# Summing v in two halves of 64 rows on Trainium2: a packed-attention kernel with a gated feed-forward

## The chip, the cores and the metric

One Trainium2 chip, one core of it. The metric is the time of one execution of the whole kernel on the device, in microseconds; lower is better. TensorE (PE) multiplies matrices and loads its weights in instructions of their own (PEld), VectorE (DVE) and ScalarE (ACT) read what it wrote to PSUM, GpSimd (POOL) works in SBUF, and SyncE (SP) issues the transfers.

## The reference

Eight batches of eight heads, 576 tokens, 64 numbers a head. 32 packing vectors p attend to the tokens, and the tokens then attend to the 32 packed vectors. The result goes through a gated feed-forward.

```
scale = 1.0 / np.sqrt(q.shape[-1])
def sm_attn(qq, kk, vv):
    s = scale * np.matmul(qq, kk.transpose(0, 1, 3, 2))
    s = s - np.max(s, axis=-1, keepdims=True)
    a = np.exp(s)
    a = a / (np.sum(a, axis=-1, keepdims=True) + 1e-09)
    return np.matmul(a, vv)
p_packed = sm_attn(p, k, v)                  # 8 x 8 x 32 x 64
out = sm_attn(q, p_packed, p_packed)         # 8 x 8 x 576 x 64
x = out.transpose(0, 2, 1, 3).reshape(B * S, H * D)
return (x @ w_a) * (x @ w_b) @ w_out         # 4608 x 512
```

## The kernel before

The batches are worked off one after the other (b = 0 to 7). Batches 0 and 1 go through a feed-forward written out slot by slot (the loops over `mm1`, lines L410 to L429); batches 2 to 7 go through a loop of periods of some 7 us each, `period`, with products at L799, the second feed-forward product at L758 as filler between them, and the weights of the next periods folded with the packed vectors in `make_g` (L813 on PE, L819 to L828 on ACT, DVE and POOL). The attention of batch b + 1 is cut into steps, which are put into the slots and periods of batch b by tables written out by hand (START, PLAN_0, PLAN, STEPS). All engines work in program order: the manual schedule keeps the order in which the code is written.

`stage1(b, e)` is the first attention of four heads (e = 0 and 1 take every other head). Its steps are: the scores (L270), the maximum (L276), the exponentials (L288), the reciprocal of the sum (`rs`, L295), the transposes that put tokens on partitions (L309 to L312, into `a1T`), and the sums of v (L319), which are scaled into `pp` (L325). It runs 16 times in all. `turned` (L256, L258) later turns `pp` into `ppT`, which `stage2` and `make_g` use.

The sums of v have five chunks of tokens, four of 128 and one of 64. For each chunk, head r of four multiplies `a1T` (128 rows by 32 columns, the weights) with `vt` (128 rows by 64 columns) and adds into partitions 32r to 32r + 31 of one bank. The profile shows each such fp32 matmul as two records, so a call leaves 40. In a form "128\*32" the array is used with 128 rows and 32 columns, in "64\*32" with 64 rows and 32 columns, in "128\*128" whole.

PSUM: `bank_pair(True)` is the one pair of banks called `s`, which the scores, the transposes, the sums of v, the second attention's scores and `turned` take in turn from batch 1 on; `bank_pair()` is one of two pairs called `m`, and `bank()` one of two single banks called `x`. So the scores of e = 1 (L270, step S1) write `s` only after DVE has read the sums of e = 0 out of it (L325). In batches 3 to 7 step S1 stands right behind `make_g`, one period after the sums of e = 0.

Of the kernel before, what the change touches and what calls it, by code (L numbers as in the profile page):

```python
# [12 lines left out]
ALU = mybir.AluOpType  # L13
# [6 lines left out]
def tile_packed_attn_gated_ffn(  # L20
# [20 lines left out]
    nc = tc.nc  # L41
    B, H, S, D = q.shape
    J = p.shape[2]
    DM, DF = w_a.shape
    DO = out.shape[1]
    P = 128
# [8 lines left out]
    NT = 5  # L55
# [37 lines left out]
    def bank():  # L93
        return ps_x.tile([P, 512], F32, name="x")

    def bank_pair(s=False):
        return ps_s.tile([P, 2, 512], F32, name="s") if s else ps_m.tile([P, 2, 512], F32, name="m")

    def work(b, name, shape, tag=None):
        if b == 0:  # L100
            return scratch.tile(shape, F32, name=name)
        return wk.tile(shape, F32, name=tag, bufs=2 if tag == "t1" else 1)
# [89 lines left out]
    def xT_cols(b, key, u, h, cols=slice(0, HS)):  # L192
        return xTs[b, key][h // R][64 * u:64 * u + 64, h % R, cols]
# [66 lines left out]
    pp, paired, a2f_of, banks_of = {}, [False], {}, {}  # L260

    def stage1(b, e):


        s = bank_pair(b or e == 0)
        first = b < 2
        parts = [(0, 0, 0, HS)] + ([(1, TR, 0, 2 * P), (1, 0, 2 * P, TR)] if first else [(1, 0, 0, HS)])
        for u, c, t, n in parts:
            for r in range(R):
                nc.tensor.matmul(  # L270
                    out=s[J * r:J * r + J, u, c:c + n], lhsT=pT[64 * u:64 * u + 64, 2 * r + e, :],
                    rhs=xT_cols(b, "k", u, 2 * r + e, slice(t, t + n)), start=True, stop=True)
        s = s[:, :, 0:HS]
        yield
        nmx = sm.tile([P, 1], F32, name="nmx")
        nc.vector.tensor_reduce(out=nmx, in_=s, axis=AXY, op=ALU.max)  # L276
        nc.vector.tensor_scalar(out=nmx, in0=nmx, scalar1=-scale, scalar2=None, op0=ALU.mult)
        if b > NB:
            yield
        a1 = work(b, f"a1_{e}", [P, S], "t1")  # L280
        rs = sm.tile([P, 1], F32, name="rs")
        if first:
            exps = [(a1, s, rs)]
        else:
            rs2 = sm.tile([P, 1], F32, name="rs2")
            exps = [(a1[:, 2 * TR:S], s[:, :, 0:2 * P], rs), (a1[:, 0:2 * TR], s[:, :, 2 * P:HS], rs2)]
        for dst, src, acc in exps:
            nc.scalar.activation(  # L288
                out=dst.rearrange("p (u t) -> p u t", u=2), in_=src, func=AF.Exp, bias=nmx, scale=scale, accum_out=acc)
        yield  # L290
        if first:
            nc.vector.tensor_scalar(out=rs, in0=rs, scalar1=1e-9, scalar2=None, op0=ALU.add)
        else:
            nc.vector.tensor_scalar(out=rs, in0=rs, scalar1=rs2, scalar2=1e-9, op0=ALU.add, op1=ALU.add)
        nc.vector.reciprocal(out=rs, in_=rs)  # L295
        yield
        a1T = work(b, f"a1T_{e}", [P, NT, P], "t2")
        rest = 2 * P if first else 0
        chunks = [P * i + ((HS + TR) * u if first else 2 * TR + 2 * P * u) for i in range(2) for u in range(2)]
        if b or e:  # L300
            pair = bank_pair(b)
            tp, tq = pair[:, 0, :], pair[:, 1, :]
        else:
            tp, tq = bank(), bank()
        if b == 0:
            chunks = [(HS + TR) * u + i for i in range(2) for u in range(2)]
        step = 1 if b else 2
        for i, c in enumerate(chunks):
            nc.tensor.transpose(tp[:, P * i:P * i + P], a1[:, c:c + step * (P - 1) + 1:step], ident)  # L309
        nc.tensor.transpose(tq[0:64, 0:P], a1[:, rest:rest + 2 * TR], ident)  # L310
        nc.scalar.copy(out=a1T[:, 0:4, :].rearrange("p i t -> p (i t)"), in_=tp)
        nc.scalar.copy(out=a1T[0:64, 4, :], in_=tq[0:64, 0:P])  # L312
        yield
        pps = bank_pair(True)[:, 0, :] if b else bank()
        vt = vts.pop((b, e))
        for i in range(NT):
            n = P if i < 4 else 64
            for r in range(R):
                nc.tensor.matmul(  # L319
                    out=pps[J * r:J * r + J, 0:D], lhsT=a1T[0:n, i, J * r:J * r + J],  # L320
                    rhs=vt[0:n, r, i, :], start=(i == 0), stop=(i == NT - 1))
        if e == 0:
            pp[b] = sm.tile([P, E + 1, D], F32, name="pp", bufs=1)
        for i in range(e, E + 1, E):
            nc.vector.tensor_scalar(out=pp[b][:, i, :], in0=pps[:, 0:D], scalar1=rs, scalar2=None, op0=ALU.mult)  # L325
        yield

    def stage2(b, e):
# [147 lines left out]
    def emit(b, plan, tasks={}):  # L476

        for name in plan.split():
# [16 lines left out]
            if what == "S":  # L495
                if e == 0:
                    st[b] = [stage1(b, 0), stage1(b, 1), stage2(b, 0), stage2(b, 1)]
                next(st[b][e])
            elif what == "s":
                next(st[b][2 + e], None)  # L500
            elif what == "r":
                next(st[b][e], None)
            elif what == "T":
                turn_p(p_nat.pop(n))
            elif what == "P":
                turned(ppT[:, b % 2:b % 2 + 2], pp.pop(b), b % 2)
            elif what in ("k", "q"):
                turn(what, n, e % 2) if b else turn_first(what, e)
            elif what == "Lk":
                load(k, "k", n, e % 2)  # L510
            elif what == "Lq":
                load(q, "q", n, e % 2)
            elif what == "Lv":
                load_v(n, e % 2)
            elif what == "Lp":
                load_p(n)
# [87 lines left out]
    for name in FIRST.split():  # L604
        what, i = name[0].lower(), int(name[1])
# [311 lines left out]
    start = slot[0]  # L917
# [16 lines left out]
    for n in range(LAST):  # L934
        b, ft = NB + n // NFT, n % NFT
# [18 lines left out]
    i, c0 = tiles[-1]  # L954
# [35 lines left out]
```

## Time and profile before

| | |
|---|---|
| median of 3 runs | 709.69 us (708.8 to 711.84) |
| span of the profiled execution | 708.6 us |
| PE busy | 698.7 us, 99% |
| weight loads (PEld) busy | 573.9 us, 81% |
| DVE busy | 447.6 us, 63% |
| ACT busy | 366.1 us, 52% |
| POOL busy | 410.8 us, 58% |

The span is that of one execution under the profiler. It lies 1.1 us under the median and just under the lowest of the three times, so a change of the span is taken as a change of the time. Busy shares are averages over the whole span; a busy PE is not one at its peak, since matmuls overlap.

### The profile page before, as it was taken

To read this page: it belongs to the slowest core of one execution; us is meant where nothing else is said; L and a number is where in the kernel's file an instruction comes from. 1 tells how busy PE (TensorE), PEld (TensorE's weight loads), DVE (VectorE), ACT (ScalarE), POOL (GpSimd) and SP (SyncE) were. 2 spreads that over 40 slices of the span, in tenths; PEclk is the share of its full clock that TensorE was granted. 3 is DMA by queue.
4 is the path that set the end of the run, shared out by engine and by line. 5 is a ranking of instruction groups with operands and counts; after the bars stand their busy time and mean duration, and the time that the engine had idled before them with its cause. 6 is when DMAs were issued, how large, how long until landed. Compare 5 with 4: busy or idle time off the path is not lost.

```text
span 708.6 us, 14190 instructions
## 1 busy us (share of the span) xinstructions
PE 698.7 (99%) x5556; PEld 573.9 (81%) x5556; DVE 447.6 (63%) x821; ACT 366.1 (52%) x735; POOL 410.8 (58%) x320
## 2 busy tenths in 40 slices
PE   8998999999999999999999999999999999999998
PEld 6486978897788888878888788788888888888886
DVE  4987655467355679665775678765785667754342
ACT  5987744544254555535554456545555446544510
POOL 0556652337244677746873589566775578856520
PEclk9999999999999999999999999999999999999999
DMA  9999954668254736456434563555245323133002
GB/s 316 382 217 317 270 98 84 191 154 286 65 131 161 173 88 168 124 138 148 138 94 123 157 175 94 123 172 154 77 113 167 105 90 120 61 122 116 1 1 74
DMA packets 176562, 102.56 MB, mean 145 GB/s; under 512 B 141936, under 2 KB 157936, under 8 KB 171120
## 3 DMA queue, kind: packets, MB, share of 16 engines
q1 hardware_dynamic: 176080, 101.08, 50.5%
q8 instruction: 43, 0.70, 0.4%
q10 hardware_dynamic: 416, 0.59, 0.2%
q14 instruction: 23, 0.19, 0.1%
HBM read 85.92 MB, written 15.73 MB: 143 GB/s over the span
## 4 chain that ended last, share of the span: by engine, by line
PE 90%; DMA 5%; ACT 2%; DVE 2%; SPq 1%; issue 0%; POOL 0%; DVEq 0%; ACTq 0%; POOLq 0%
PE x L758 37%; PE m L799 29%; PE m L410 8%; PE m L436 5%; PE x L813 5%; DMA raw<-in_moe_w_b_dram 2%; PE s L319 2%; PE s L334 1%; PE s L270 1%; DMA vt<-in_v_dram 1%; PE s L309 1%; DMA nat<-in_k_dram 1%; DMA wr<-w_kept 1%; PE x L389 1%; ACT raw L201 1%; DVE w_ab L212 0%
## 5 line engine op out<-in xcount | busy, mean ns | idle before, releaser
L758 PE MATMUL x<-wo,h_hi 128*128 128x512 f32 (+1 forms) x776 | 249.4, 391 | 0.2 <-ACT gs L819 0.2
L91 POOL TENSOR_TENSOR h_lo<-asb,h_hi 128x576 fp32r<-128x576 f32 x96 | 140.2, 1461 | 91.1 <-ACT h_hi L844 44.7
L758 PEld LDWEIGHTS x<-wo,h_hi 128*128 128x128 f32 x776 | 140.8, 188 | 22.3 <-ACT gs L819 1.2
L758 PE MATMUL x<-wo,h_lo 128*128 128x512 f32 (+1 forms) x388 | 152.1, 392 | 0.0
L91 POOL TENSOR_TENSOR G_lo<-gs,G_hi 128x640 fp32r<-128x640 f32 x72 | 113.0, 1575 | 30.8 <-ACT G_hi L834 30.5
L758 PEld LDWEIGHTS x<-wo,h_lo 128*128 128x128 f32 x388 | 72.9, 188 | 11.7
L91 POOL TENSOR_TENSOR A_lo<-gs,A_hi 128x256 fp32r<-128x256 f32 x36 | 27.1, 754 | 89.5 <-ACT A_hi L822 89.4
L881 DVE TENSOR_TENSOR d<-m,d 128x576 f32<-128x576 f32 (+1 forms) x73 | 54.0, 740 | 34.7 <-ACT d L877 33.9
L894 DVE TENSOR_TENSOR asb<-m,d 128x288 f32<-128x288 f32 x72 | 32.5, 451 | 66.7 <-ACT c L890 65.1
L890 ACT COPY c<-m 128x288 f32<-128x288 f32 x72 | 28.8, 399 | 78.3 <-PE m L799 78.3
L768 DVE TENSOR_TENSOR part<-x,part 128x512 f32<-128x512 f32 (+1 forms) x65 | 44.1, 678 | 38.8 <-PE x L758 38.8
L819 ACT COPY gs<-x 128x512 f32<-128x512 f32 x36 | 21.1, 587 | 83.3 <-PE x L813 80.2
L799 PE MATMUL m<-tx_hi,G_hi 128*128 128x288 f32 x216 | 63.8, 296 | 0.0
L799 PE MATMUL m<-tx_hi,G_lo 128*128 128x288 f32 x216 | 63.7, 295 | 0.0
L799 PE MATMUL m<-tx_lo,G_hi 128*128 128x288 f32 x216 | 63.3, 293 | 0.0
L834 ACT CAST G_hi<-gs 128x640 fp32r<-128x640 f32 x72 | 52.2, 730 | 15.1 <-POOL gs L828 14.5
L877 ACT COPY d<-m 128x576 f32<-128x576 f32 (+1 forms) x73 | 46.6, 639 | 20.2 <-PE m L799 18.6
L844 ACT CAST h_hi<-asb 128x576 fp32r<-128x576 f32 x72 | 49.0, 680 | 11.5 <-DVE asb L908 11.5
L799 PEld LDWEIGHTS m<-a_hi,G_hi 128*128 128x128 f32 x144 | 27.0, 187 | 31.9 <-issue 17.4
L828 POOL TENSOR_TENSOR gs<-gs 128x512 f32<-128x512 f32 x36 | 46.7, 1297 | 2.6 <-DVE gs L825 2.5
L799 PE MATMUL m<-a_hi,G_hi 128*128 128x288 f32 x144 | 47.1, 327 | 0.0
L410 PE MATMUL m<-a_hi,ghi 128*128 128x288 f32 x192 | 43.3, 307 | 2.8 <-ACT asb L422 2.8
(170 smaller groups left out, 1541.7 us busy)
## 6 DMA issues: line engine op xcount, KB each, us to landing
wr<-w_kept SPq DMA_DIRECT2D x36, 1024.0 KB, 5.1
nat<-in_k_dram SPq DMA_DIRECT2D x56, 144.0 KB, 5.2
nat<-in_q_dram SPq DMA_DIRECT2D x56, 144.0 KB, 5.3
vt<-in_v_dram SPq DMA_DIRECT2D x28, 256.0 KB, 3.7
out_dram<-part SPq DMA_DIRECT2D x27, 256.0 KB, 2.0
raw<-in_moe_w_a_dram SPq DMA_DIRECT2D x12, 512.0 KB, 9.3
raw<-in_moe_w_b_dram SPq DMA_DIRECT2D x12, 512.0 KB, 9.8
raw<-in_moe_w_out_dram SPq DMA_DIRECT2D x12, 512.0 KB, 6.4
```

The costliest lines, as they stand in the source:

```text
L91: return eng.tensor_tensor(out=dst, in0=src, in1=hi.bitcast(F32), op=ALU.subtract)
L410: nc.tensor.matmul(out=ps[:, half, 0:HS], lhsT=gt[:, kt, ft % 4, cols], rhs=at[:, kt, HS * half:HS * half + HS], start=(n == 0 and kt == 0 ...
L436: nc.tensor.matmul(out=o[:, cols], lhsT=ht[:, c0:c0 + P], rhs=wt[:, cols], start=(ft == 0 and n == 0), stop=(ft == NFT - 1 and n == 2))
L758: nc.tensor.matmul(out=o[:, cols], lhsT=ht[:, c0:c0 + P], rhs=wt[:, cols], start=(ft == fts[0] and n == 0), stop=end)
L768: nc.vector.tensor_tensor(out=parts[i][:, cols], in0=o[:, cols], in1=parts[i][:, cols], op=ALU.add)
L799: nc.tensor.matmul(out=bank[:, n % 2, 0:HS], lhsT=g, rhs=t, start=(first and i == 0), stop=(i == 2), skip_group_check=True)
L813: nc.tensor.matmul(out=gps[e][J * r:J * r + J, :], lhsT=ppT[rows, 2 * (b % 2), r, :], rhs=w[rows, r, :], start=True, stop=True)
L828: nc.gpsimd.tensor_tensor(out=gs[:, 2:4].rearrange("p a u f -> p a (u f)"), in0=gs[:, 0:2].rearrange("p a u f -> p a (u f)"), in1=s2.unsqu ...
L834: nc.scalar.copy(out=G_hi[:, n % 3], in_=gs[:, 1:6, n % 2])
L844: nc.scalar.copy(out=view(h_hi[ft]), in_=src)
L877: nc.scalar.copy(out=d[:, both], in_=X[:, both, 0:HS])
L881: nc.vector.tensor_tensor(out=d[:, both], in0=V[:, both, 0:HS], in1=d[:, both], op=ALU.add)
```

## The change

The sums of v take the four full chunks in halves of 64 rows: rows 0 to 63 add into the first bank of a pair, rows 64 to 127 into the second, and the last chunk of 64 rows into the first. DVE then scales the second bank's sums into a piece of `a1T` (which the matmuls have read by then) and adds that while it scales the first bank's. In batch 0 the sums take `s` and an `m` pair instead of two `x` banks. Lines behind the change stand four further down (L799 is L803, L813 is L817).

```
-        pps = bank_pair(True)[:, 0, :] if b else bank()
+        pps = bank_pair(b > 0 or e == 0)
         vt = vts.pop((b, e))
         for i in range(NT):
-            n = P if i < 4 else 64
             for r in range(R):
-                nc.tensor.matmul(
-                    out=pps[J * r:J * r + J, 0:D], lhsT=a1T[0:n, i, J * r:J * r + J],
-                    rhs=vt[0:n, r, i, :], start=(i == 0), stop=(i == NT - 1))
+                for g in range(2 if i < 4 else 1):
+                    rows = slice(64 * g, 64 * g + 64)
+                    nc.tensor.matmul(
+                        out=pps[J * r:J * r + J, g, 0:D], lhsT=a1T[rows, i, J * r:J * r + J],
+                        rhs=vt[rows, r, i, :], start=(i == 0), stop=(i == NT - 1 - g))
         if e == 0:
             pp[b] = sm.tile([P, E + 1, D], F32, name="pp", bufs=1)
+        pg = a1T[:, 0, 0:D]
+        nc.vector.tensor_scalar(out=pg, in0=pps[:, 1, 0:D], scalar1=rs, scalar2=None, op0=ALU.mult)
         for i in range(e, E + 1, E):
-            nc.vector.tensor_scalar(out=pp[b][:, i, :], in0=pps[:, 0:D], scalar1=rs, scalar2=None, op0=ALU.mult)
+            nc.vector.scalar_tensor_tensor(
+                out=pp[b][:, i, :], in0=pps[:, 0, 0:D], scalar=rs, in1=pg, op0=ALU.mult, op1=ALU.add)
```

On PE, at the sums of e = 0 of batch 3 (a row is one instruction or several alike, with the semaphores that it waits for), the kernel before has:

```order
L319 MATMUL s<-vt,t_3415 32x64 [waits DMAHW7_49,PE_49,Activation_49]
L319 MATMUL s<-vt,t_3415 32x64 x7
L319 MATMUL s<-vt,t_3415 32x64 [waits DMAHW0_49]
L319 MATMUL s<-vt,t_3415 32x64 x7
L319 MATMUL s<-vt,t_3415 32x64 [waits DMAHW1_49]
L319 MATMUL s<-vt,t_3415 32x64 x3
L813 MATMUL x<-wr,ppT 32x512 [waits DMAHW0_49,DVE_49]
L813 MATMUL x<-wr,ppT 32x512 x3
L813 MATMUL x<-wr,ppT 32x512 [waits DVE_49]
L813 MATMUL x<-wr,ppT 32x512 x3
L270 MATMUL s<-xT_3087,pT 32x288 [waits DVE_49,PE_49]
```

and the changed kernel, at the same place:

```order
L320 MATMUL s<-vt,t_3551 32x64 [waits DMAHW7_49,PE_49,Activation_49]
L320 MATMUL s<-vt,t_3551 32x64 x15
L320 MATMUL s<-vt,t_3551 32x64 [waits DMAHW0_49]
L320 MATMUL s<-vt,t_3551 32x64 x15
L320 MATMUL s<-vt,t_3551 32x64 [waits DMAHW1_49]
L320 MATMUL s<-vt,t_3551 32x64 x3
L817 MATMUL x<-wr,ppT 32x512 [waits DMAHW0_49,DVE_49]
L817 MATMUL x<-wr,ppT 32x512 x3
L817 MATMUL x<-wr,ppT 32x512 [waits DVE_49]
L817 MATMUL x<-wr,ppT 32x512 x3
L270 MATMUL s<-xT_3223,pT 32x288 [waits DVE_49,PE_49]
```

Nothing changes place: 20 matmuls become 36, and the scores of e = 1 (L270) still wait for DVE.

On DVE, at the same place, the kernel before has (`m`, `c`, `d` and `asb` belong to the period's products):

```order
L325 TENSOR_SCALAR pp<-s,rs 128x64 [waits DVE_49,PE_49]
L325 TENSOR_SCALAR pp<-s,rs 128x64
L907 TENSOR_TENSOR m<-m,c_3337 128x288
L908 TENSOR_TENSOR asb<-m,d 128x288 [waits DVE_49]
L824 TENSOR_TENSOR gs<-x,gs 128x256 [waits Activation_49,Pool_49]
```

and the changed kernel:

```order
L326 TENSOR_SCALAR t_3551<-s,rs 128x64 [waits DVE_49,PE_49,Activation_49]
L328 SCALAR_TENSOR_TENSOR pp<-s,rs,t_3551 128x64 [waits DVE_49]
L328 SCALAR_TENSOR_TENSOR pp<-s,rs,t_3551 128x64
L911 TENSOR_TENSOR m<-m,c_3473 128x288
L912 TENSOR_TENSOR asb<-m,d 128x288 [waits DVE_49]
L828 TENSOR_TENSOR gs<-x,gs 128x256 [waits Activation_49,Pool_49]
```

One instruction more stands ahead of the period's own work, and the next one waits for it. For e = 1 there is one L328 instead of two.

## Rows read from the trace of the kernel before

**Rows 1.** The page: the span, the granted clock, the chain's shares

```profile
span 708.6 us, 14190 instructions
...
PEclk9999999999999999999999999999999999999999
...
PE 90%; DMA 5%; ACT 2%; DVE 2%; SPq 1%; issue 0%; POOL 0%; DVEq 0%; ACTq 0%; POOLq 0%
```

**Rows 2.** Who waited for the sums of v: us, times

```profile
  PEld s L270: 3.6, 5
```

**Rows 3.** Timeline, one call of batch 1: start us, us, engine, records merged

```profile
76.47 0.90 PE L319 MATMUL s<-vt,t 128*32 128x64 f32 x40
...
76.55 0.52 PE L319 MATMUL s<-vt,t 128*32 128x64 f32 x24
...
77.05 0.26 PE L319 MATMUL s<-vt,t 64*32 64x64 f32 x4
...
77.13 0.24 PE L319 MATMUL s<-vt,t 64*32 64x64 f32 x4
77.30 0.33 PE L247 MATMUL x<-ident,p_nat 128*128 128x128 f32 x1
```

**Rows 4.** Timeline, and by line (ns min/median/max): other 64\*32 matmuls

```profile
138.39 0.43 PE L389 MATMUL m<-w_ab,ppT 64*32 64x256 f32 x3
...
237.67 0.47 PE L334 MATMUL s<-xT,ppT 64*32 64x288 f32 x8
...
L334 PE MATMUL s<-xT,ppT x240: 402/403/428, 16.2 to 583.8; 64*32 64x288 f32 x120
...
L389 PE MATMUL m<-w_ab,ppT x48: 375/376/401, 126.0 to 152.2; 64*32 64x256 f32 x48
```

**Rows 5.** Timeline, batch 3, around the sums of e = 0

```profile
208.09 1.04 PE L813 MATMUL x<-wr,ppT 64*32 64x512 f32 x12
208.34 0.48 DVE L325 TENSOR_SCALAR pp<-s,rs 128x64 f32<-128x64 f32 x2 [0.96 <-PE s L319]
...
208.94 0.21 PEld L270 LDWEIGHTS s<-xT,pT 64*32 64x32 f32 x16 [0.71 <-PE s L319]
...
209.22 0.46 DVE L908 TENSOR_TENSOR asb<-m,d 128x288 f32<-128x288 f32 x1
...
210.13 0.42 DVE L824 TENSOR_TENSOR gs<-x,gs 128x256 f32<-128x256 f32 x1 [0.45 <-ACT A_hi L821]
...
210.52 0.30 PE L799 MATMUL m<-a_hi,A_hi 128*128 128x288 f32 x1
```

**Rows 6.** Timeline, batch 7, around the sums of e = 0

```profile
541.58 0.48 DVE L325 TENSOR_SCALAR pp<-s,rs 128x64 f32<-128x64 f32 x2 [0.96 <-PE s L319]
...
542.17 0.21 PEld L270 LDWEIGHTS s<-xT,pT 64*32 64x32 f32 x16 [0.71 <-PE s L319]
```

**Rows 7.** Groups by line: count, busy us, mean ns, idle before it

```profile
L908 DVE TENSOR_TENSOR asb<-m,d 128x288 f32<-128x288 f32 x72 | 32.9, 457 | 2.5
```

**Rows 8.** Timeline, batch 3, behind the sums of e = 1

```profile
226.49 0.24 DVE L325 TENSOR_SCALAR pp<-s,rs 128x64 f32<-128x64 f32 x1
226.97 0.42 DVE L824 TENSOR_TENSOR gs<-x,gs 128x256 f32<-128x256 f32 x1 [0.24 <-ACT A_hi L821]
...
230.89 0.37 PEld L256 LDWEIGHTS s<-ident,pp 128*128 128x128 f32 x2
```

**Rows 9.** Timeline, batches 1 and 2, behind sums of v

```profile
81.05 0.76 DVE L425 TENSOR_TENSOR asb<-m,asb 128x576 f32<-128x576 f32 x1 [1.59 <-PE m L410]
...
138.74 0.47 DVE L325 TENSOR_SCALAR pp<-s,rs 128x64 f32<-128x64 f32 x2
...
139.70 0.49 PE L270 MATMUL s<-xT,pT 64*32 64x288 f32 x7
```

**Rows 10.** Timeline, batch 0, behind the sums of e = 1

```profile
14.86 0.28 DVE L325 TENSOR_SCALAR pp<-x,rs 128x64 f32<-128x64 f32 x1 [0.35 <-PE x L319]
...
15.19 0.20 PEld L256 LDWEIGHTS x<-ident,pp 128*128 128x128 f32 x2
```

## The prediction

> **What bounds the kernel now.** I read the page first: the span is 708.6 us, PE's granted clock is full in every slice (the upper of its two levels, 2.4 GHz), and 90% of the chain that ended last is PE [rows 1]. So time that PE saves or waits counts nearly one for one, and other engines count where PE waits for them. The changed lines touch PE and DVE. The view of the sums' own line names one PE instruction that waits behind the sums: the score matmuls L270, 5 times, 3.6 us of idle weight loader [rows 2]. I then took one call apart in the timeline, and after it every place behind the 16 calls.
>
> **The call on PE.** A call leaves 40 records [rows 3], ten groups of four, the four heads side by side on their own columns. Four such records of one group start within 0.02 us. The group at 76.55 to the group that ends the 24 records is six groups: 0.52 less one record's 0.22 leaves 0.30 between first and last start, less 0.02 within the last group, over five steps: 0.056 us a group. The first step is 76.55 - 76.47 = 0.08, since no weights are loaded ahead. So the eight full groups start at 0, 0.08 and then every 0.056, the last at 0.416. The first 64-row group starts at 77.05, 0.58 behind the first, or 0.17 behind the last full one instead of 0.056: when the array's shape goes from 128\*32 to 64\*32, the work in it runs out first. The second 64-row group again needs 0.08 (77.13, at 0.66), and the next whole-array matmul starts at 77.30.
>
> **What the change does there.** All records become 64\*32, and the shape no longer changes inside the call. If two row halves run side by side, a chunk still takes two groups (now of eight records), the ninth group starts at 0.08 + 7 x 0.056 = 0.47 and the tenth at 0.53, against 0.66: 0.13 us saved. That eight run side by side is shown by L334, which has the same pattern of four column places and two row halves: eight records in 0.47 us, where one lasts up to 0.428 [rows 4], so eight start within 0.04 to 0.05 us. That just fits into a step of 0.056. The other limit is how fast fp32 matmuls come in: where PE's queue had run low, three records of L389, up to 0.401 long, took 0.43 [rows 4], so the second and third started some 13 to 15 ns behind the one ahead; a chunk of eight needs 0.11 us, as long as its two groups. I take 0.13 us a call, with 0.09 as the bound if intake holds the last chunk up by a few records, and negative values among the rivals. Behind the call PE goes on: in ten calls of batches 3 to 7 with L813, of the same shape, whose last four matmuls stand behind row half 0 and so gain the same.
>
> The Trainium skill, in "TensorE: Matmul & The Clock Gate", section "Wait — 56ns, not 53.3ns?", says that start to start of matmuls never drops below about 25 ns however small they are. By it 72 records would take an estimated 1.8 us a call, 1.1 us more than now, and the kernel some 20 us more. The trace disagrees: 40 records of a call start within 0.66 us, 17 ns each, with four of them within 0.02 [rows 3].
>
> **What the change does on DVE.** Before, e = 0 has two scalings, 0.48 us together, and one alone is 0.28 [rows 5, 10], so an independent second starts 0.20 behind the first. After, a scaling into `pg` (0.28) comes first; the next waits for its end. Dependent neighbours on DVE stand 2.5 us / 72 = 0.035 apart [rows 7]. Then two scale-and-adds, 0.20 apart, the last 0.28 long: 0.28 + 0.035 + 0.48 = 0.80 against 0.48, so +0.32 us. The trace has no scale-and-add on 128x64 with a bank as input. I bound it by the scaling's 0.24 below [rows 8], and above by L824, a two-input operation on 128x256 out of PSUM, 0.42 [rows 5]; it is nearest to the scaling, being as narrow, so 0.28.
>
> **Where that reaches PE, call by call.**
> Batches 3 to 7, e = 0 (five calls): L270 starts at 208.94, 0.12 behind the end of L325 (208.34 + 0.48 = 208.82), and in batch 7 at 542.17, 0.11 to 0.12 behind 542.06 [rows 5, 6]. A fixed distance to DVE, 0.7 us after the loader's last work: DVE's reading of `s` releases it, although the view puts the wait down to the sums. L813 ahead of it has its last matmuls running until about then (208.09 + 1.04 = 209.13 with its drain), which is why it cost PE almost nothing so far. After the change the sums end 0.13 earlier, DVE 0.32 - 0.13 = 0.19 later, and PE, which is ready 0.13 earlier, waits 0.32 in all. Net +0.19 each, +0.95 us. Behind it L908 is 0.19 later too; its bank is next needed at 210.52, 0.8 behind its end, and L824 waits 0.45 for ACT [rows 5], so nothing else is late.
> Batches 3 to 7, e = 1 (five calls): -0.13 each, -0.65 us. DVE's extra 0.32 lies partly in L824's idle 0.24, the rest ahead of work that PE wants much later; `pp` itself is wanted at 230.89, 4.2 us behind the scaling [rows 8].
> Batch 2, e = 0: DVE comes to L325 at 138.74 whatever PE does, since it is at other work until then; `s` would be free at 139.21 + 0.32 = 139.53, L270's weights could load 0.12 behind it as in batch 3, and L270's matmuls start at 139.70 now [rows 9]. PE would be ready at 139.57 and waits about what it gained: 0.
> Batch 1 (two calls) and batch 2, e = 1: -0.13 each, -0.39 us; behind the first of them DVE stands idle for 1.59 us [rows 9], and behind the other two, too, for longer than 0.32, which hides the extra work there.
> Batch 0: the calls stand back to back and save some 0.3 on PE, but L256 starts 0.05 behind the last scaling (14.86 + 0.28) [rows 10], so DVE decides: its first chain starts 0.13 earlier and has 0.32 more in it, the second starts 0.20 behind the first's last instruction, and ends near 15.20 instead of 15.14: +0.06.
>
> Sum: 0.95 - 0.65 + 0 - 0.39 + 0.06 = -0.03 us on the span of 708.6. The median stands 1.1 us above it and moves alike: 709.7 us.
>
> **The rivals.**
> (a) DVE's part costs nothing: L270 follows something else than L325, or the new operations overlap. For it: the view names PE for the wait. Against: the same 0.12 us behind DVE in both calls shown. Then 16 x 0.13 = 2.1 us are won: 707.6.
> (b) DVE's part costs more: a scale-and-add of 0.42, and the second 0.34 behind the first. That is 0.28 more, on the five calls of e = 0 and in batch 0: +1.7 us, 711.4. With intake at the 0.09 bound besides, 712.0.
> (c) The slower side: the two row halves do not run side by side when matmuls are this short. Then a call has 18 groups, the last at 0.08 + 16 x 0.056 = 0.98 instead of 0.66: +0.32 a call. Nine calls (e = 1 of batches 3 to 7, batches 1 and 2) give 9 x 0.32 = 2.9, the five of e = 0 give 0.64 each, 3.2, batch 0 some 0.9: +7 us, 716.7. Against it stands L334; for it, that L334 is 288 columns wide where these are 64, so the trace shows no overlap at this pace. It decides from the point where a group of eight takes over 0.075 us in place of 0.056: 0.08 + 7 x 0.075 + 0.056 is today's 0.66.
> (d) PE takes in no more than it does now, 17 ns a record on average: 72 records are 1.22 us, +0.56 a call, and with DVE's part some +11 us, 720. The Trainium skill's floor, if it held, would be this rival at a higher price (an estimated 730).
>
> **How the numbers follow.** The forecast (PE's gain eaten by DVE in five places) has 0.62, (a) 0.12, (b) 0.12, (c) 0.08, (d) 0.03, and 0.03 are left for what I do not see. The time is 709.7. Measured medians of the kernel scatter by 1 us or so, and about 0.5% (3.5 us) is what a measurement can tell from no change. The range reaches to (a) and (b), 707.3 to 712.6, and leaves out (c) and (d). Faster by over 0.5% has no mechanism, since all of PE's gain is 2.1 us: 0.03. Slower by over 0.5% is (c), (d) and a rest: 0.13. Within: 0.84.
>
> **What would show it.** Right: the sums' groups of eight at steps of 0.056, the tenth group 0.53 behind the first, no pause inside the call; L328 ending 0.80 behind the start of L326; L270 still 0.12 behind L328, some 0.2 us later against the call's start plus what stands between; the calls of e = 1 shorter by 0.13 to L817. Wrong: groups of eight at 0.1 us or more, L270 following PE, or a wait at L803 for L912 or L885 that was not there.

## The result, and the profile after

| | before | after |
|---|---|---|
| median of 6 runs each | 709.38 us (708.80 to 711.84) | 713.38 us (712.69 to 717.92) |
| ratio, 95% interval | | 1.0064 [1.0042, 1.0085] |
| span of the profiled execution | 708.6 us | 713.4 us |
| PE busy / DVE busy | 698.7 / 447.6 us | 702.9 / 452.3 us |

The kernel became slower by 4.0 us between the medians. Each timed run is 1.8 us longer than its span, and the six spans of after are 713.4, 711.6, 710.9, 716.1, 711.2 and 711.5. So the profiled execution of after lies above its median, and so does that of before, 708.6 + 1.8 = 710.4; the differences below are taken stage by stage.

The page of after, its span and the chain, for [rows 1]:

```profile
span 713.4 us, 15235 instructions
...
PE 96%; DMA 2%; DVE 1%; issue 1%; ACT 0%; SPq 0%; DVEq 0%; ACTq 0%
```

PE is still nearly all of the chain; nothing else has become the bound.

**The call on PE.** The timeline of after, the call at 77.13 that answers to the one at 76.47 [rows 3]; then, for the call at 562.15, four answers for windows that end at 562.40, 562.53, 562.71 and 562.94. The last number of a row counts the records that had begun by then.

```profile
77.13 0.97 PE L320 MATMUL s<-vt,t 64*32 64x64 f32 x72
78.04 0.33 PE L247 MATMUL x<-ident,p_nat 128*128 128x128 f32 x1
...
562.15 0.45 PE L320 MATMUL s<-vt,t 64*32 64x64 f32 x32
562.15 0.62 PE L320 MATMUL s<-vt,t 64*32 64x64 f32 x38
562.15 0.78 PE L320 MATMUL s<-vt,t 64*32 64x64 f32 x58
562.15 0.97 PE L320 MATMUL s<-vt,t 64*32 64x64 f32 x72
```

A record lasts 0.22 us, so the last of 72 starts about 0.75 us behind the first; the last of 40 did so after 0.68. The prediction had the last group begin at 0.53. The rows also show where it went: the first 32 records (16 matmuls, two chunks) start within 0.45 - 0.22 = 0.23 us. The next six take 0.17 us, and after them 20 records (10 matmuls) take 0.78 - 0.62 = 0.16 us, 16 ns a matmul. Record by record the trace has the first four groups of eight at 0, 0.08, 0.135 and 0.19 us, 6.6 ns between neighbours; then a pause until 0.33 us with two records in it; then matmuls at 0.330, 0.347, 0.364, 0.380 and so on, 16.7 ns apart.

**Around the sums of e = 0.** The timeline of after in batch 3, which answers to [rows 5]:

```profile
209.48 0.92 PE L320 MATMUL s<-vt,t 64*32 64x64 f32 x68
...
210.57 0.28 DVE L326 TENSOR_SCALAR t<-s,rs 128x64 f32<-128x64 f32 x1 [1.08 <-PE s L320]
210.89 0.47 DVE L328 SCALAR_TENSOR_TENSOR pp<-s,rs,t 128x64 f32<-128x64 f32 x2
211.29 0.45 DVE L911 TENSOR_TENSOR m<-m,c 128x288 f32<-128x288 f32 x1
211.48 0.21 PEld L270 LDWEIGHTS s<-xT,pT 64*32 64x32 f32 x16 [1.06 <-PE x L817]
211.51 0.72 PE L270 MATMUL s<-xT,pT 64*32 64x288 f32 x16 [0.18 <-DVE pp L328]
...
212.16 0.40 PE L803 MATMUL m<-a_hi,G_hi 128*128 128x288 f32 x1
```

DVE's chain lasts from 210.57 to 210.89 + 0.47 = 211.36: 0.79 us, where the prediction had 0.80. L270's weights load 0.12 behind that. But DVE starts 1.09 behind the call instead of 0.97, and L803 2.68 instead of 2.24. The view of L270's own line, on what the loader waited for (us, times), for [rows 2]:

```profile
  PE x L817: 5.4, 6
...
  DVE pp L328: 0.4, 2
```

The wait grew from 3.6 us in five places to 5.4 us in six, and the name beside it changed from one work of PE to another.

The same distances in all ten calls of batches 3 to 7, in us behind a call's first record:

| | before | predicted | after |
|---|---|---|---|
| start of the last record | 0.684 | about 0.55 | 0.753 to 0.770 |
| e = 0: DVE starts | 0.97 | 0.84 | 1.07 to 1.09 |
| e = 0: DVE ends | 1.44 | 1.63 | 1.86 to 1.89 |
| e = 0: next product (L799, now L803) | 2.24 | 2.43 | 2.66 to 2.68 |
| e = 1: next product | 1.69 | 1.56 | 1.78 to 1.84 |

So e = 0 lost 0.42 five times, e = 1 some 0.12 five times, and batch 2 about 0.08 twice: 2.9 us. From batch 2's first call to the end, after needs 573.55 us and before 570.83, 2.7 more. The rest of the loss lies ahead of that call.

**Batch 0.** The timeline of after, PE:

```profile
13.39 0.97 PE L320 MATMUL s<-vt,a1T 64*32 64x64 f32 x72
14.19 0.71 PE L320 MATMUL m<-vt,a1T 64*32 64x64 f32 x48
16.66 0.50 PE L320 MATMUL m<-vt,a1T 64*32 64x64 f32 x24 [1.75 <-issue]
17.09 0.66 PE L153 MATMUL m<-ident,qn 128*128 128x128 f32 x4
```

In the middle of the second call PE stands for 1.75 us and waits for no semaphore. The table of stretches (us of each engine with instructions in brackets, then the granted clock and the DMA) shows what follows:

```profile
17.00:19.00 2.00, 1.28 (x23) 0.72 (x22) 0.99 (x3) 1.22 (x3) 0.00 (x0) 1.00 1.06 389
19.00:21.00 2.00, 2.00 (x33) 0.68 (x33) 0.82 (x2) 2.00 (x4) 0.00 (x0) 0.51 1.06 385
21.00:23.00 2.00, 2.00 (x7) 1.01 (x4) 2.00 (x3) 1.27 (x3) 1.20 (x1) 0.64 1.04 383
```

Behind it the clock is granted at the lower of its two levels, 1.2 GHz, for some 3.4 us. Yet of all this only 77.13 - 76.47 = 0.66 us is left at batch 1's first call [rows 3], and runs below whose batch 0 is that of before reach it anywhere from 74.58 (e8) to 76.73 us (e5). The DMA engines are busy for 0.95 to 1.00 of each stretch up to there (20 us long, the last 17), so that the transfers are the likely bound.

### The profile page after: what moved, and what is told of

Same layout as the page of the kernel before. It is cut to its first block, busy times and chain, and to the rows that moved or that the text cites. A ratio compares the mean times of both kernels' runs of the same rounds, so it can differ in the third digit from the quotient of the medians.

```text
span 713.4 us, 15235 instructions
## 1 busy us (share of the span) xinstructions
PE 702.9 (99%) x6068; PEld 577.6 (81%) x6068; DVE 452.3 (63%) x837; ACT 366.3 (51%) x735; POOL 410.7 (58%) x320
## 4 chain that ended last, share of the span: by engine, by line
PE 96%; DMA 2%; DVE 1%; issue 1%; ACT 0%; SPq 0%; DVEq 0%; ACTq 0%
PE x L762 37%; PE m L803 29%; PE m L414 11%; PE x L817 5%; PE m L440 4%; PE s L320 2%; PE x L393 1%; PE s L338 1%; PE s L270 1%; PE m L590 1%; DMA qn<-in_q_dram 1%; DMA vt<-in_v_dram 1%; PE s L309 1%; PE m L393 0%; PE s L310 0%
## 5 line engine op out<-in xcount | busy, mean ns | idle before, releaser
L803 PE MATMUL m<-tx_hi,G_hi 128*128 128x288 f32 x216 | 63.8, 296 | 0.0
L803 PE MATMUL m<-tx_hi,G_lo 128*128 128x288 f32 x216 | 63.7, 295 | 0.0
L803 PE MATMUL m<-tx_lo,G_hi 128*128 128x288 f32 x216 | 63.3, 293 | 0.0
L803 PEld LDWEIGHTS m<-a_hi,G_hi 128*128 128x128 f32 x144 | 27.0, 187 | 31.9 <-issue 17.4
L803 PE MATMUL m<-a_hi,G_hi 128*128 128x288 f32 x144 | 47.0, 326 | 0.0
L911 DVE TENSOR_TENSOR m<-m,c 128x288 f32<-128x288 f32 x72 | 33.3, 463 | 17.2 <-PE m L803 15.4
```

The source lines that it names most:

```text
L803: nc.tensor.matmul(out=bank[:, n % 2, 0:HS], lhsT=g, rhs=t, start=(first and i == 0), stop=(i == 2), skip_group_check=True)
L911: nc.vector.tensor_tensor(out=v, in0=v, in1=c2, op=ALU.add)
```

## The experiments

Two accounts of the call were open. By the **intake**, PE takes in fp32 matmuls one by one, at a pace set by their number and not by their shape, and only some stand ready at a call's start. By the **row halves**, two halves of the array hinder each other. For DVE the prediction's account (L270 follows DVE) stood against the view, which names PE. Ratios are to runs of before taken with each group; "e = 0" and "e = 1" are medians over batches 3 to 7.

**e1: before, with each matmul in two halves of 32 columns from batch 1 on** (40 matmuls of whole rows, DVE reads two banks in the same operations):

```
... (the pair of banks)
-                nc.tensor.matmul(
-                    out=pps[J * r:J * r + J, 0:D], lhsT=a1T[0:n, i, J * r:J * r + J],
-                    rhs=vt[0:n, r, i, :], start=(i == 0), stop=(i == NT - 1))
+                for g in range(2 if b else 1):
+                    o, c = (pps[:, g, 0:32], slice(32 * g, 32 * g + 32)) if b else (pps[:, 0:D], slice(0, D))
+                    nc.tensor.matmul(
+                        out=o[J * r:J * r + J], lhsT=a1T[0:n, i, J * r:J * r + J],
+                        rhs=vt[0:n, r, i, c], start=(i == 0), stop=(i == NT - 1))
... (DVE's operands)
```

> Before, but from batch 1 on each matmul of the sums takes 32 columns of v, not 64, the two column halves in two banks: 40 matmuls a call instead of 20, full rows, DVE as before. Theory I (matmuls come in at 0.0167 us each once the first 16 are used up): the call gets longer though its rows are whole, last record at 0.80 to 0.95 us (before 0.684, the change 0.76), L270 and L799 0.1 to 0.25 later, 1.5 to 3 us slower than before. Theory R (row halves hinder each other): no row halves here, the groups are shorter, last record at 0.68 or less, time within 0.5 us of before.

Measured: 713.28 us, 1.0052 [1.0036, 1.0068], a loss of 3.7 us [2.6, 4.8] where 1.5 to 3 were expected. The call in its timeline (batch 1):

```profile
75.79 1.14 PE L321 MATMUL s<-vt,t 128*32 128x32 f32 x80
```

The last record starts 0.942 us behind the first, L803 comes 0.26 later for e = 0 and 0.25 for e = 1. No row halves are in it, each matmul does half as much, and still the call is 0.26 longer. The trace of PE's sequencer, which hands PE its instructions, has a mark for this: a semaphore stands behind the four full chunks, and in most calls it is reached 0.16 us after the call's start in before (16 matmuls ahead of it), and 0.55 us in e1, in e3, in e4 and in the change (32 ahead). So the number of matmuls sets it, whatever part of the array they use. Each matmul brings its own weight loads, so the loader could be what sets the pace. But when the sequencer reaches the mark, 15 of the 32 weight loads ahead of it have begun in before, and 60 of 64 in the change, 58 of 64 in e1; of the matmul records ahead of it 12 of 32, 57 of 64 and 54 of 64. In the longer calls the loader and the array have all but caught up with the sequencer and don't hold it back. That is the intake; the row halves fall.

**e2: before's matmuls with the change's DVE operations** (all on one bank, so the sums come out twice as large):

```
+        pg = a1T[:, 0, 0:D]
+        nc.vector.tensor_scalar(out=pg, in0=pps[:, 0:D], scalar1=rs, scalar2=None, op0=ALU.mult)
         for i in range(e, E + 1, E):
-            nc.vector.tensor_scalar(out=pp[b][:, i, :], in0=pps[:, 0:D], scalar1=rs, scalar2=None, op0=ALU.mult)
+            nc.vector.scalar_tensor_tensor(
+                out=pp[b][:, i, :], in0=pps[:, 0:D], scalar=rs, in1=pg, op0=ALU.mult, op1=ALU.add)
```

> Before's matmuls, with the change's DVE operations, which both read the one bank (so that the sums come out twice as large). Both theories: the call on PE as before (last record 0.684), DVE's chain 0.32 longer, L270 of batches 3 to 7 0.32 later in five places, the calls of e = 1 unchanged: +1.6 us. If DVE's part costs nothing: 0.

Measured: 712.43 us, 1.0044 [1.0029, 1.0058]. Timeline, batch 3:

```profile
206.71 0.84 PE L319 MATMUL s<-vt,t 128*32 128x64 f32 x36
...
207.74 0.28 DVE L325 TENSOR_SCALAR t<-s,rs 128x64 f32<-128x64 f32 x1 [1.02 <-PE s L319]
208.06 0.48 DVE L327 SCALAR_TENSOR_TENSOR pp<-s,rs,t 128x64 f32<-128x64 f32 x2
...
208.65 0.21 PEld L270 LDWEIGHTS s<-xT,pT 64*32 64x32 f32 x16 [1.09 <-PE x L816]
```

PE's call is as before (0.684), and L270 still comes 0.376 later: 0.32 for the chain and 0.06 because DVE starts at 1.03 instead of 0.97. Its first operation now writes a piece of `a1T` and waits for a third semaphore, ACT's, though ACT's copy into `a1T` has ended 0.7 us or more ahead of the call; at batch 2's first call, where it waits for two, it starts at 0.97 as before. e = 1 did not move (1.688). So DVE holds L270 up, whatever the view names, and costs 5 x 0.376 = 1.9 us there. The loss as a whole, 3.1 us [2.1, 4.1], is more than that and than the 1.6 expected; the profiled execution lost 2.3 from batch 2 on, and what the rest is isn't shown.

**e3: the change's matmuls with before's DVE operations**, which read the first bank alone (rows 64 to 127 of four chunks are left out of the result):

```
-        pg = a1T[:, 0, 0:D]
-        nc.vector.tensor_scalar(out=pg, in0=pps[:, 1, 0:D], scalar1=rs, scalar2=None, op0=ALU.mult)
         for i in range(e, E + 1, E):
-            nc.vector.scalar_tensor_tensor(
-                out=pp[b][:, i, :], in0=pps[:, 0, 0:D], scalar=rs, in1=pg, op0=ALU.mult, op1=ALU.add)
+            nc.vector.tensor_scalar(out=pp[b][:, i, :], in0=pps[:, 0, 0:D], scalar1=rs, scalar2=None, op0=ALU.mult)
```

> The change's matmuls, with before's DVE operations on the first bank alone (the sums leave out rows 64 to 127 of four chunks). Theory I and R: last record at 0.76, L270 and the products some 0.10 to 0.12 later in ten places, four calls of batches 1 and 2 some 0.07: +1.4 us. Together with the DVE part about the whole of the change from batch 1 on.

Measured: 711.43 us, 1.0027 [1.0012, 1.0042], a loss of 1.9 us [0.9, 3.0] for an expected 1.4. The last record starts at 0.753 to 0.759 (0.783 in one call of ten), L800 0.04 to 0.07 later for e = 0 and 0.09 to 0.13 for e = 1. PE's half of the change costs time by itself, where the prediction had it gain 0.13 a call.

**e4: the change with the halves outside the heads** (four matmuls on rows 0 to 63, then four on rows 64 to 127):

```
-            for r in range(R):
-                for g in range(2 if i < 4 else 1):
+            for g in range(2 if i < 4 else 1):
+                for r in range(R):
```

> The change, with the four heads of the lower row half ahead of the four of the upper one in each chunk. Theory I: as many matmuls, so last record at 0.74 to 0.78 and the time of the change, 713.4 within 0.7. Theory R, if alternating the halves is what costs: last record near 0.55, 2 to 3 us under the change.

Measured: 714.68 us, 1.0068 [1.0051, 1.0086], 0.6 above the band; the calls read as in the change (0.758). The order within a chunk does not matter for a call.

**e5 and e6: the change from batch 1 on alone, and in batch 0 alone** (`split = b > 0`, or `b == 0`, chooses between the two forms of sums and scaling).

> The change from batch 1 on, batch 0 as before (whole rows, single banks, before's DVE). Theory I (each later call costs PE 0.08 to 0.12 in place of saving 0.13, and DVE's longer chain holds L270 up in five places): 5 x (0.42 + 0.12) + 4 x 0.08 = 3.0 us slower than before, no stall in batch 0. Theory S (the loss comes from the stall and the low clock in batch 0): within 1 us of before.

Measured: 713.41 us, 1.0049 [1.0036, 1.0062], a loss of 3.5 us [2.6, 4.4] for an expected 3.0; calls as in the change, no pause in batch 0.

> The change in batch 0 alone, the other batches as before. Theory I: the stall of 1 to 2 us in the second call of batch 0 comes back, and the lower clock level behind it, but the transfers that bound the first 60 us hide most of it: 0 to 1.5 us slower than before, all calls from batch 1 on as before. Theory S: 3 to 4 us slower.

Measured: 710.66 us, 1.0006 [0.9992, 1.0021]. The pause is there, 1.12 us long, but the loss is 0.4 us [-0.6, 1.5]. The change loses its time from batch 1 on.

**e7: before, with the first two chunks alone in halves of 32 columns, from batch 1 on** (28 matmuls, one bank). It asks whether 28 matmuls still fit into what stands ready, or each added matmul has its price:

```
+                for g in range(2 if b and i < 2 else 1):
+                    c = slice(32 * g, 32 * g + 32) if b and i < 2 else slice(0, D)
                     nc.tensor.matmul(
-                        out=pps[J * r:J * r + J, 0:D], lhsT=a1T[0:n, i, J * r:J * r + J],
-                        rhs=vt[0:n, r, i, :], start=(i == 0), stop=(i == NT - 1))
+                        out=pps[J * r:J * r + J, c], lhsT=a1T[0:n, i, J * r:J * r + J],
+                        rhs=vt[0:n, r, i, c], start=(i == 0 and g == 0), stop=(i == NT - 1), skip_group_check=True)
```

> Before, but from batch 1 on the first two chunks in two matmuls of 32 columns of v each, in the one bank: 28 matmuls a call, whole rows, DVE as before. Theory I in its form with a stock (16 matmuls stand ready, the others come every 0.0167): the 28th is there at about 0.53, before it is wanted, so the call stays at 0.68 to 0.72 and the time within 0.7 us of before. Theory L (each further matmul costs the same, 0.26 / 20 = 0.013 by the run with 40): last record at 0.79, L799 0.10 later in ten places, 1.2 to 1.6 us slower.

Measured: 711.44 us, 1.0025 [1.0015, 1.0034], a loss of 1.8 us [1.1, 2.4]; last record at 0.802, the next product 0.12 later for both. The expectation of some 0.7 fell, and the call came out as the rival with a price for each added matmul had it (0.79): the 16 half-width matmuls of the first two chunks have started after 0.28 us, and then the starts thin out here too. The semaphore behind the full chunks, with 24 matmuls ahead of it, is reached at 0.42: from 24 to 32 it is (0.55 - 0.42) / 8 = 17 ns a matmul. What is ready at the start covers some 16 matmuls, however small they are. The full chunks' last records tell the same: 0.44 us behind the call's start with 16 matmuls (before), 0.55 with 24, and 0.66 with 32, in e1 and in the change alike.

**e8: before, with e = 0's two copies of `pp` written by one operation:**

```
-        for i in range(e, E + 1, E):
-            nc.vector.tensor_scalar(out=pp[b][:, i, :], in0=pps[:, 0:D], scalar1=rs, scalar2=None, op0=ALU.mult)
+        n = 2 - e
+        nc.vector.tensor_scalar(
+            out=pp[b][:, e:E + 1:E, :], in0=pps[:, 0:D].unsqueeze(1).broadcast_to([P, n, D]), scalar1=rs, scalar2=None,
+            op0=ALU.mult)
```

> Before, with the two scalings of e = 0 in one DVE operation that writes both copies: DVE's reading of the bank ends some 0.13 us earlier. If L270's weight loads follow DVE: they start some 0.13 earlier against the call's start (1.43 instead of 1.56), but its matmuls only a little, since L813 holds the array until then: time within 0.5 us of before. If L270 follows PE: its loads stay at 1.56.

Measured: 709.04 us, 0.9990 [0.9977, 1.0003]. Timeline, batch 3:

```profile
206.73 0.35 DVE L325 TENSOR_SCALAR pp<-s,rs 128x128 f32<-128x128 f32 x1 [0.96 <-PE s L319]
...
207.14 0.34 PEld L270 LDWEIGHTS s<-xT,pT 64*32 64x32 f32 x16 [0.52 <-DVE pp L325]
```

DVE ends 0.13 sooner, L270's weights load 0.19 sooner, now 0.05 behind DVE's end, and the view names DVE. Only DVE's work was changed, so that settles who releases L270; why the distance shrank from 0.12 isn't known. The next product comes 0.07 sooner, 0.3 us over five calls, which the timing can't tell from nothing.

**e9: before, with the sums of batch 0 alone in halves of 32 columns** (whole rows, one bank, 40 matmuls a call):

```
+                for g in range(1 if b else 2):
+                    c = slice(0, D) if b else slice(32 * g, 32 * g + 32)
                     nc.tensor.matmul(
-                        out=pps[J * r:J * r + J, 0:D], lhsT=a1T[0:n, i, J * r:J * r + J],
-                        rhs=vt[0:n, r, i, :], start=(i == 0), stop=(i == NT - 1))
+                        out=pps[J * r:J * r + J, c], lhsT=a1T[0:n, i, J * r:J * r + J],
+                        rhs=vt[0:n, r, i, c], start=(i == 0 and g == 0), stop=(i == NT - 1), skip_group_check=True)
```

> Before, with the sums of v of batch 0 alone split into two groups of 32 columns (whole rows, one bank, 40 matmuls a call in place of 24), everything from batch 1 on and VectorE as before. Theory S (the pause in batch 0's second call comes from the number of TensorE's instructions there, which have to be fetched): a pause of 0.4 to 2 us in or behind batch 0's second call without a semaphore waited for, and instruction packets around it. Rival Q (the pause belongs to sums over halves of rows): the call runs through in about 0.95 us and no pause shows. Either way the time is within 1 us of before, and the calls of batches 1 to 7 read 0.684 us to the last record.

Measured: 710.32 us, one run (before 709.17 beside it). Timeline, batch 0:

```profile
13.28 1.69 PE L321 MATMUL x<-vt,a1T 128*32 128x32 f32 x119
15.12 0.75 PE L321 MATMUL x<-vt,a1T 128*32 128x32 f32 x41
```

Here too the calls break off, 0.35 us from start to start, with PE idle for 0.15 of it, less than the 0.4 to 2 expected. But the place is the same to one record: behind record 119, and behind record 72 + 48 = 120 in the change, e3, e4, e6 and e10. So the pause belongs to a place in PE's instructions, which before never reaches within these sums (it ends them at 80 records), and not to the row halves. In the change, e3, e4, e6, e9 and e10 PE goes on 1.3 to 1.6 us after a transfer of 16 KB of instructions has ended, though that end lies anywhere from 13.5 us (e9) to 15.4 us (the change) into the execution. That fits a wait for instructions, but no run was built to move that transfer, so it is not shown.

**e10: the change with one scale-and-add that writes both copies:**

```
-        for i in range(e, E + 1, E):
-            nc.vector.scalar_tensor_tensor(
-                out=pp[b][:, i, :], in0=pps[:, 0, 0:D], scalar=rs, in1=pg, op0=ALU.mult, op1=ALU.add)
+        twice = lambda t: t.unsqueeze(1).broadcast_to([P, 2 - e, D])
+        nc.vector.scalar_tensor_tensor(
+            out=pp[b][:, e:E + 1:E, :], in0=twice(pps[:, 0, 0:D]), scalar=rs, in1=twice(pg), op0=ALU.mult, op1=ALU.add)
```

> The change with one scale-and-add for e=0 that writes both copies, in place of two. Theory: TensorE's call stays at 0.755 us to the last record; VectorE ends 0.1 to 0.3 us sooner in the first call of batches 3 to 7, so that L270 starts at 1.75 to 1.9 us behind the call's start in place of 2.02, which gives back 0.5 to 1.3 us of the change's 3.7: 1.7 to 3.4 us above before. Rival (one op over twice the columns that reads two banks takes as long as two): L270 at 2.0 and the time as the change's, 3 to 4 us above before.

Measured: 713.33 us, 1.0058 [1.0044, 1.0072]. Timeline, batch 3 (the call starts at 208.09):

```profile
209.18 0.28 DVE L326 TENSOR_SCALAR t<-s,rs 128x64 f32<-128x64 f32 x1 [1.08 <-PE s L320]
209.50 0.35 DVE L328 SCALAR_TENSOR_TENSOR pp<-s,rs,t 128x128 f32<-128x128 f32 x1
...
209.97 0.21 PEld L270 LDWEIGHTS s<-xT,pT 64*32 64x32 f32 x16 [0.94 <-PE x L817]
```

L270 comes 1.88 to 1.91 behind the call instead of 2.01 to 2.03, again 0.12 behind DVE. The stretch from batch 2 to the end lost 2.4 us instead of 2.7. The time as a whole is not told apart from the change's; its excess of 4.1 us [3.1, 5.1] lies above the 1.7 to 3.4 expected. With PE's call unchanged, a leaner DVE can't make up for it.

## Why the prediction was wrong

It was 709.7 us with a range up to 712.6, and 713.4 came.

- **The step that failed is the first term: "a chunk of eight needs 0.11 us, as long as its two groups. I take 0.13 us a call".** That holds for the first two chunks, which start at steps of 0.056 us. From the seventeenth matmul on, PE takes one every 16.7 ns, a chunk needs 8 x 16.7 = 0.13 us, and where the ready ones run out it pauses besides. The records of the full chunks have all started after some 0.66 us, where the prediction had the last group begin at 0.42 and so end at 0.46: 0.20 more. The slower pace makes only some 2 x 0.02 of that. The pause makes some 0.08 (the third chunk gets going at 0.33 instead of 0.25), and a matmul's second record now follows its first by 0.11 instead of 0.056. The gain at the end of the call (no change of shape) is real, and the last chunk follows 0.01 behind the full ones instead of 0.15, but the full chunks end 0.22 later than in before. So the call became 0.07 us longer instead of 0.13 shorter. e1 and e7 show the same loss without row halves, and e3 without DVE's part.
- **The evidence was read too generously.** The step of 13 to 15 ns came from three records [rows 4], and the step of 0.056 us was read from 24 records [rows 3], 12 matmuls, which is within what stands ready. Before needed one matmul per 0.056 / 2 = 0.028 us, so the intake never showed; the change asked for one per 0.014.
- **The chain on DVE was right:** 0.79 for a predicted 0.80, the scale-and-add at 0.28. L270 follows it by 0.12 (e2, e10; 0.05 in e8), and rival (a) is out. What was missed is 0.06 us at its start, the third semaphore. Its part in the loss, 5 x 0.376 = 1.9 us, was to be eaten up by PE's gain in the calls without it; there was none.
- **Call by call**, against the prediction: e = 0 lost 0.42 for 0.19 (five times), e = 1 lost 0.12 for a gain of 0.13 (five), batch 1 twice and batch 2's e = 1 lost 0.07 for a gain of 0.13, and batch 2's e = 0 0.09 for nothing: 1.15 + 1.25 + 0.6 + 0.1 = 3.1 of the 3.7 us by which the time missed. In batch 2's first call the prediction had DVE come to the sums at its own time; it follows PE there too, at 1.03 instead of 0.97. At e = 1 the products lose more than the call's 0.07: L817's first record comes 0.69 to 0.82 behind the call's start, and L813's came at 0.61. That it waits for the same intake is likely, but no run tested it.
- **The rivals.** The scale-and-add cost what the forecast took, so (b) is out. (c) is out: eight records on eight places start within 0.05 us, at the predicted step. (d) named the right cause at 0.56 a call; the price was an eighth of it, because 16 matmuls stand ready, what comes after costs 8 ns a record, not 17, and the change of shape is gone. The floor of 25 ns that the Trainium skill states in "TensorE: Matmul & The Clock Gate", section "Wait — 56ns, not 53.3ns?", is not borne out: neighbours start 6.6 ns apart on different places.
- **The base** was the profiled execution's span plus 1.1; its own time was 710.4, 1.8 above its span and 1.0 above the median. That shifts nothing between before and after.

**What stays open.** The calls account for some 3.0 us (with batch 1's two) of 4.0 to 4.5 (the medians, the ratio). Batch 0 adds 0.4 by e6, within its interval of nothing. In batch 1 the second call waits for `vt` in some profiles (0.68 and 0.40 us in after, in e10 together some 0.9, in e8, whose work on PE is that of before, 0.44, in before and e9 nothing); how often it does in runs without a profile isn't known. Why there is a pause ahead of the steady 16.7 ns isn't known either.

## What to carry to other kernels

Splitting matmuls to fill the array halves the work of each but doubles their number. Before doing so, compare the rate at which the split form would have to start with the best rate that the trace shows over a long run of such instructions, not over the first few. And a wait that the view puts down to PE can be DVE's: a constant distance behind the end of one engine's work, across several places, tells more than the name in the bracket, and a run that shortens that work alone settles it (e8).

## What the runs showed of the hardware

- fp32 matmuls of two records are taken in at 16.7 ns each over a run of 16 (6.6 ns between records inside a group of eight); about 16 stand ready at a call's start. 64x64 on half the rows and 128x32 on half the columns come in at the same pace: 32 of either are past PE's sequencer after 0.55 us.
- Two neighbouring DVE operations on 128x64 take 0.48 us, one on 128x128 0.35, for scalings and scale-and-adds alike (e8, e10).
- In the first 20 us, 16 or 20 more matmuls a call brought a pause of 0.15 to 1.75 us at the same place in the program. Behind the longest PE ran at a granted clock of 0.51 and then 0.64 (stretches of 2 us), its 64x288 matmuls at up to 0.68 us instead of 0.43; behind 1.48 us (e4) the clock fell too, to 0.50 and then 0.69, and behind 1.14 us (e10) it stayed at 1.00.
- With the same work ahead on PE, DVE's first operation starts 1.03 us behind the sums' start where it waits for three semaphores and 0.97 where it waits for two, although the third had come long before (e2).
- Where the matmuls change from the form 128\*32 to 64\*32, the next record starts 0.15 us behind the last one; inside 128\*32 a group starts 0.04 us behind the one ahead (before).
